# Attention and a feed-forward layer on one core: values of two pairs in one block, three products for the last rows, eight float32 pairs, first loads in another order

## The chip, the core and the metric

The kernel runs on one core of one Trainium2 chip. The metric is the device time of one execution in microseconds (us), before any host work. The engines are named as the profile names them: PE (TensorE, with PEld for its weight loads), DVE (VectorE), ACT (ScalarE), POOL (GpSimd) and SP (SyncE), whose queue issues nearly all transfers.

## The reference

```python
B, H, S, D = 8, 8, 576, 64                       # q, k, v, f
scores = (q @ k^T) / sqrt(D)
cum = cumsum(log(clip(f, 1e-4, 1)))              # per batch and head
scores = where(causal, scores + cum[i] - cum[j], -1e9)
attn = exp(scores - max); attn /= attn.sum() + 1e-9
x = (attn @ v) -> [B*S, H*D] = [4608, 512]
h = x @ w_in                                     # [4608, 2048]
out = (max(h, 0) + alpha * min(h, 0)) @ w_out    # [4608, 512]
```

All is float32. w_in and w_out come as 64-bit numbers, whose conversion on DVE, ACT and POOL is part of the kernel.

## The kernel before

The 64 heads are worked on as 32 pairs, n = 4 b + p: two heads of one batch. A pair's 576 rows are cut into four tiles of 128 rows per head (`tile`, i = 0 to 3, as wide as the causal mask lets them be: 128 (i + 1) columns) and the last 64 rows of each head, which share one set of 128 partitions (`tail`): two groups g of 288 columns.

A score tile goes PE (products into one of 8 PSUM banks) -> DVE (`red`, L628 and L553: adds the mask, scales, takes the row's extreme) -> ACT (exponential with its sum, L518) -> PE (transposes, L531 and L650) -> ACT or DVE (`evac`, L526 and L527: into the tiles eT1, eT2, eT4). `values` (L660 to L680) multiplies them with v: for the rows 0 to 255 (r = 0) and 256 to 575 (r = 1), 64 columns of head 0 into partitions 0 to 63 of a bank and 64 of head 1 into 64 to 127. `quotients` (L587) turns the nine row sums of a pair into reciprocals (L592, L593), transposes them (L596), writes them to DRAM (L602) and reads them back as rows (L604); the fourth pair does this on PE (`quick`). The quotient times the values (L695) is x, which ACT and POOL split into two parts (L697, L699).

Float32 products take several passes of PE. So only the first NN = 6 pairs compute their scores in float32 (`load_0`: tiles q and k of 66 rows, the last two rows of which add the cumulated decay). The later ones use split numbers (`load_n`): KA and QA hold 128 rows, KB and QB 68, so that each product becomes two in a fast format (KA with QA, KB with QB); rounding is done at L424, the remainders on POOL at L474 and L478, and the rows of the decay come from cq in DRAM. Two sets of these four tiles exist (rQ), and one raw q and k (rrq, rrk).

The first feed-forward layer (`ffn1`, b = 0 to 8; b = 8 holds the last 64 rows of all heads) multiplies x of four pairs with w_in in three products each (L726), and ACT and DVE bring the result through four buffers hs to DRAM (L740). w_in is loaded and converted by `load_w_in` and `split64` (L298 to L321). The second layer (`ffn2`, from 741.7 us on) works with seven products in place of eight for blocks of two by two. x tiles are kept in seven buffers (rx).

The order of work is not left to the hardware. Every piece is an `op` with an engine, an expected time, a key and the buffers that it needs. `Plan.run` walks through time and gives each engine the piece that can start first, at equal start the one with the lowest key, and writes out each engine's instructions in this order. Attention has keys of about 10 n, FFN1 1e6: it fills gaps. Each engine, and SP's queue too, works strictly in this order, so a piece that was expected early and comes late holds up what stands behind it. `change_a` frees the memory of the float32 tiles (p0) when their last scores are done and turns it into a second pair of eT1 and eT2 buffers.

Of the kernel before, what the change touches and what calls it, by code (L numbers as in the profile page):

```python
# [18 lines left out]
NP = H // 2  # L19
# [5 lines left out]
NN = 6  # L25
NS = 10
HURRY = 25
CONV0, CONV = 36, 2.2
# [154 lines left out]
def attention_moe(  # L183
# [21 lines left out]
    cq = dram.tile([2, B * H, 2, S], F32, name="cq")  # L205
    c0 = dram.tile([2, 2 * H, S], F32, name="c0")
# [21 lines left out]
    def ring(pool, n, shape, dt, name):  # L228
# [7 lines left out]
    rQ = Ring(Store([(sp.tile([128, QW], F32R, name=f"QA{i}"), sp.tile([68, 1280], F32R, name=f"QB{i}"),  # L236
                      sp.tile([128, 2 * S], F32R, name=f"KA{i}"), sp.tile([68, 2 * S], F32R, name=f"KB{i}"))
                     for i in range(2)]))
# [15 lines left out]
    sel = sp.tile([9, 6, 128], F32, name="sel")  # L254
    mask = sp.tile([128, 928], BF16, name="mask")
    warm = sp.tile([1, 1], F32, name="warm")

# [5 lines left out]
    wbf = p0.tile([128, 512], BF16, name="wbf")  # L263

    def change_a():
        ctx_0.close()
        p1 = ctx_a.enter_context(tc.tile_pool(name="pa", bufs=1, reuse_waits="tile"))
        for r, shape, name in ((rT1, [128, 384], "eT1b"), (rT2, [128, 4, 320], "eT2b")):
            for i in range(2):
                r.store.free.append((plan.t, len(r.store.items)))  # L270
                r.store.items.append(p1.tile(shape, F32, name=f"{name}{i}"))
# [17 lines left out]
    def c_dve(n):  # L289
        return 75 + n / 0.96  # L290
# [114 lines left out]

    o_zero = op("POOL", 400, zeros, -96)
# [23 lines left out]
    def load_0(n, bqk):  # L430
# [3 lines left out]
        ld = [op("SP", 450, lambda: sy.dma_start(bqk.t[0][0:64], qq[b, p, 0:64]), -99 if n < 2 else key, (), [bqk], kb=304),  # L434
              op("SP", 450, lambda: sy.dma_start(bqk.t[1][0:64], kk[b, p, 0:64]), -99 if n < 2 else key, (), [bqk], kb=288)]
# [22 lines left out]
    def load_n(n, bQ):  # L458
# [14 lines left out]
        for i, (a0, a1) in enumerate(pieces(QW, 4)):  # L473
            rdy.append(op("POOL", c_po(a1 - a0), lambda a0=a0, a1=a1: po.tensor_tensor(  # L474
                QA()[64:128, a0:a1], bq.t[64:128, a0:a1], QA()[64:128, a0:a1].bitcast(F32), ALU.subtract),
                kc, [qc[i // 2], qb], [bq, bQ]))
        for i, (a0, a1) in enumerate(pieces(2 * S, 4)):
            rdy.append(op("POOL", c_po(a1 - a0), lambda a0=a0, a1=a1: po.tensor_tensor(  # L478
                KB()[0:64, a0:a1], bk.t[0:64, a0:a1], KA()[0:64, a0:a1].bitcast(F32), ALU.subtract),
                kc, [kc_[i // 2]], [bk, bQ]))  # L480
        q2 = lambda: QB()[66:68].rearrange("p (h s) -> p h s", h=2)[:, :, 0:S].bitcast(F32)
# [5 lines left out]
        return rdy  # L487

    def attention(n):
# [6 lines left out]

        if n >= NN:
            bQ = Buf(rQ)
            rdy, held = [[load_n(n, bQ)] * 2] * 2, [bQ]
# [36 lines left out]
        def tail(st):  # L536
# [3 lines left out]
            for g in range(2):  # L540
# [9 lines left out]
                s = op("PE", 2 * len(qf) * c_s(288), prods, st + 0.6 * g, rdy[0][1] + rdy[1][1], [bS] + held)  # L550

                def red(bS=bS, ks=ks, g=g):
                    ve.tensor_tensor_reduce(out=bt.t[:, ks], in0=bS.t[:, :288], in1=mask[:, 0:288] if g else mask[:, 288:576],  # L553
# [3 lines left out]
                prev = op("DVE", c_dve(288) + 60, red, st + 0.6 * g, [s, o_mask, prev], [bS, bt, bst])  # L557
# [29 lines left out]
        def quotients(key):  # L587
# [3 lines left out]
            def rec():  # L591
                ve.tensor_scalar_add(su(), su(), 1e-9)  # L592
                ve.reciprocal(su(), su())  # L593

            q_ = op("DVE", 160, rec, key, sums, [bst])
# [64 lines left out]
        def values(r, st):  # L660

            bP, w_ = Buf(rP), R[r][1]

            def pv():
                both = []
                for h in range(2):
# [6 lines left out]
                for c, pair in enumerate(zip(*both)):  # L673
                    for h, (j, q0, q1, m) in enumerate(pair):
                        mm(bP.t[64 * h : 64 * h + 64, q0:q1], bv.t[:, j, h], m, c == 0, c == len(both[0]) - 1)

            ns = 3 * c_m4(320) + c_m4(192) + c_m4(64) if r else c_m4(256) + c_m4(128)

            pvo = op("PE", ns + 95, pv, st, e1 + e2[0] + e2[1] + [e4, o_zero, l_v], [bP, bv] + (bT2 + [bT4] if r else bT1))
            xs_ops[r].append(op("ACT", c_act(w_), lambda: ac.activation(bxs[r].t, bP.t[:, :w_], AF.Copy), st, [pvo], [bP, bxs[r]]))  # L680
# [7 lines left out]
        for r in range(2):  # L688
            values(r, k0 + 9.6 - hurry)
        quotients(k0 + 11 - hurry)  # L690
        bx, xo = Buf(rx), []
        for r in range(2):
            t0, w_ = R[r]
            st = k0 + 11.5 - hurry
            mu = op("DVE", c_dve(w_), lambda r=r, t0=t0, w_=w_: ve.tensor_tensor(bxs[r].t, bxs[r].t, bri.t[:, t0 : t0 + w_], ALU.mult),  # L695
                    st, xs_ops[r] + ri_ops, [bxs[r], bri])
            xh = op("ACT", c_acs(256), lambda r=r, t0=t0: ac.activation(  # L697
                bx.t[:, 0, t0 : t0 + 256], bxs[r].t[:, 0:256], AF.Copy), st, [mu], [bxs[r], bx])
            xl = op("POOL", c_po(256), lambda r=r, t0=t0: po.tensor_tensor(  # L699
                bx.t[:, 1, t0 : t0 + 256], bxs[r].t[:, 0:256], bx.t[:, 0, t0 : t0 + 256].bitcast(F32), ALU.subtract), st, [xh], [bxs[r], bx])  # L700
            xo += [xh, xl]
            x_late.extend((mu, xh, xl))
        xt_ops.append(op("SP", 400, lambda: sy.dma_start(xt[p, :, 64 * b : 64 * b + 64], bxs[1].t[:, 256:320]), k0 + 11.6, [mu], [bxs[1]], kb=32))
        x_late.append(xt_ops[-1])
        x_ops[b, p] = [bx] + xo
# [46 lines left out]
    o_one = [op("POOL", 2500, lambda i=i: ones(po, i), 0.5 + i, [s_0[-1]] + x_ops[0, 0][1:]) for i in range(2)]  # L752
# [3 lines left out]
    op("-", 0, change_a, 0, s_0)  # L756
# [292 lines left out]
```

## Time and profile before

| | |
|---|---|
| median of 3 runs | 1105.41 us (1100.49 to 1105.73) |
| profiled execution | 1105.64 us, span 1103.9 us |
| mean granted clock of PE | 0.992 |
| PE busy | 1093.6 us, 99% |
| DVE, ACT, POOL busy | 770.9, 673.0, 267.1 us |
| DMA | 169.54 MB, mean 154 GB/s |

The busy shares say which engine has no room; stretches of 25 us say where this holds, since the attention stage (up to about 600 us) mixes with FFN1 and the last third is the second layer alone. In rows in order of time, two numbers lead: the start and how long the row lasted, and a row joins neighbours of one line and engine under the form of the first. Matrix products overlap at their ends, so the distance between starts is what a product costs, not its own duration.

### The profile page before, as it was taken

The numbers are of one execution on the slowest core, as the hardware profiler recorded it, in microseconds if no ns is written. First come the engines' busy times: TensorE is split into PE (matmuls) and PEld (weight loads), VectorE is DVE, ScalarE is ACT, GpSimd is POOL, SyncE is SP. The second block draws the span as 40 slices with busy tenths as digits, with TensorE's granted clock in tenths as the row PEclk, the third lists the DMA queues.
The fourth block names the chain that finished last, engine by engine and source line by source line (L and its number), as shares of the span: only waits on it lengthen the run. The fifth ranks groups of instructions, "written<-read, shape, count | busy, mean of one in ns | idle before, by whom it ended". The sixth has DMA issues, their size and how long they took to land.

```text
span 1103.9 us, 20650 instructions
## 1 busy us (share of the span) xinstructions
PE 1093.6 (99%) x7281; PEld 953.5 (86%) x7281; DVE 770.9 (70%) x1772; ACT 673.0 (61%) x1580; POOL 267.1 (24%) x340
## 2 busy tenths in 40 slices
PE   8999999999999999999999999999999999999998
PEld 5777878888888888888787888889999999999998
DVE  4887786565555654654532688469989898998994
ACT  4888777677658764774763465555455464646451
POOL 3346574444534533444401000000000000000000
PEclk7999999999999999999999999999999999999999
DMA  4667665646555646565322666454344344443521
GB/s 109 182 183 224 208 194 155 191 139 203 169 168 161 183 150 185 149 185 172 119 71 98 213 210 214 158 183 143 117 152 131 122 130 134 134 134 116 147 65 39
DMA packets 104748, 169.54 MB, mean 154 GB/s; under 512 B 15790, under 2 KB 61637, under 8 KB 104644
## 3 DMA queue, kind: packets, MB, share of 16 engines
q1 hardware_dynamic: 104228, 167.96, 49.5%
q8 instruction: 57, 0.93, 0.4%
q14 instruction: 47, 0.39, 0.1%
q10 hardware_dynamic: 416, 0.27, 0.1%
HBM read 111.04 MB, written 49.04 MB: 145 GB/s over the span
## 4 chain that ended last, share of the span: by engine, by line
PE 97%; DMA 1%; DVE 1%; POOL 0%; issue 0%; SPq 0%; DVEq 0%
PE bank L324 89%; PE bank L531 8%; DMA k<-in_kk_dram 0%; POOL KB L478 0%; DMA rk<-in_kk_dram 0%; PE bank L596 0%; PE bank L650 0%; DMA q<-e 0%; DVE st L592 0%; DVE xs L695 0%; DVE hs L983 0%; DVE es L628 0%; DVE hs L986 0%; DVE hs L985 0%; SPq L337 0%
## 5 line engine op out<-in xcount | busy, mean ns | idle before, releaser
L324 PE MATMUL bank<-xx,wi 128*128 128x512 f32 x1728 | 424.4, 395 | 0.0
L324 PEld LDWEIGHTS bank<-xx,wi 128*128 128x128 f32 x1728 | 318.2, 189 | 61.4
L738 DVE SCALAR_TENSOR_TENSOR hs<-bank,sa,hs 128x512 f32<-128x512 f32 x96 | 71.6, 745 | 82.5 <-ACT hs L736 82.4
L478 POOL TENSOR_TENSOR KB<-rk,KA 64x288 fp32r<-64x288 f32 x104 | 89.1, 878 | 158.9 <-DVE KA L424 102.3
L324 PE MATMUL bank<-wot,xx 128*128 128x256 f32 x1008 | 123.9, 283 | 0.0
L324 PE MATMUL bank<-wi,xx 128*128 128x256 f32 x1008 | 123.9, 283 | 0.0
L324 PEld LDWEIGHTS bank<-wot,xx 128*128 128x128 f32 x1008 | 122.3, 192 | 0.0
L324 PEld LDWEIGHTS bank<-wi,xx 128*128 128x128 f32 x1008 | 122.3, 192 | 0.0
L518 ACT ACTIVATE e<-e,st 128x512 f32<-128x512 f32 (+2 forms) x160 | 109.4, 685 | 14.9 <-DVE st L553 10.0
L736 ACT ACTIVATE hs<-bank,ab 128x512 f32<-128x512 f32 x96 | 65.9, 687 | 71.8 <-PE bank L324 71.0
L628 DVE CUSTOM_DVE_ANT_0 e<-bank,mask 128x512 f32<-128x512 f32 (+1 forms) x128 | 76.7, 620 | 36.5 <-PE bank L324 17.9
L474 POOL TENSOR_TENSOR QA<-rq,QA 64x304 fp32r<-64x304 f32 x104 | 91.4, 910 | 28.6 <-DVE QA L424 27.0
L324 PE MATMUL bank<-KA,QA 128*128 128x288 f32 (+4 forms) x312 | 92.9, 335 | 0.0
L324 PE MATMUL bank<-KB,QB 68*128 68x288 f32 (+4 forms) x312 | 88.1, 316 | 0.0
L628 DVE CUSTOM_DVE_ANT_0 es<-bank,mask 128x256 f32<-128x256 f32 (+1 forms) x128 | 43.6, 353 | 58.7 <-PE bank L324 36.3
L531 PE MATMUL bank<-ident,e 128*128 128x128 f32 x576 | 82.6, 275 | 0.0
L699 POOL TENSOR_TENSOR xx<-xs,xx 128x256 fp32r<-128x256 f32 x64 | 49.1, 786 | 136.9 <-ACT xx L697 133.6
L531 PEld LDWEIGHTS bank<-ident,e 128*128 128x128 f32 x576 | 69.6, 142 | 10.0 <-issue 0.9
L527 ACT ACTIVATE eT<-bank 128x384 f32<-128x384 f32 (+2 forms) x136 | 61.9, 487 | 22.7 <-PE bank L531 20.2
L518 ACT ACTIVATE es<-es,st 128x256 f32<-128x256 f32 (+1 forms) x128 | 57.2, 449 | 26.3 <-DVE st L628 25.4
L942 ACT ACTIVATE xx<-gx 128x1024 fp32r<-128x1024 f32 x48 | 50.8, 1058 | 31.1 <-PE bank L324 15.3
L945 DVE TENSOR_TENSOR xx<-gx,xx 128x1024 fp32r<-128x1024 f32 x48 | 58.6, 1221 | 8.1 <-ACT xx L942 8.1
(136 smaller groups left out, 1740.5 us busy)
## 6 DMA issues: line engine op xcount, KB each, us to landing
hd<-hs SPq DMA_DIRECT2D x144, 256.0 KB
wx<-hd SPq DMA_DIRECT2D x47, 512.0 KB
rq<-in_qq_dram SPq DMA_DIRECT2D x26, 608.0 KB
rk<-in_kk_dram SPq DMA_DIRECT2D x26, 576.0 KB
hr<-hd SPq DMA_DIRECT2D x25, 512.0 KB
vr<-in_vv_dram SPq DMA_DIRECT2D x32, 320.0 KB
wr<-in_w_in_dram SPq DMA_DIRECT2D x16, 512.0 KB
wr<-in_w_out_dram SPq DMA_DIRECT2D x16, 512.0 KB
```

The costliest lines, as they stand in the source:

```text
L324: pe.matmul(o, lhsT, rhs, start=start, stop=stop)
L474: rdy.append(op("POOL", c_po(a1 - a0), lambda a0=a0, a1=a1: po.tensor_tensor(QA()[64:128, a0:a1], bq.t[64:128, a0:a1], QA()[64:128, a0:a1] ...
L478: rdy.append(op("POOL", c_po(a1 - a0), lambda a0=a0, a1=a1: po.tensor_tensor(KB()[0:64, a0:a1], bk.t[0:64, a0:a1], KA()[0:64, a0:a1].bitca ...
L518: ex = op("ACT", c_exp(w), lambda: ac.activation(bt.t[:, :w], bt.t[:, :w], AF.Exp, bias=lo()[:, col : col + 1], scale=-1.0, accum_out=su() ...
L527: return op("ACT", c_act(w), lambda: ac.activation(dst(), src(), AF.Copy), key, deps, [bank] + bufs)
L531: pe.transpose(t[:, c : c + 128], src[:, 128 * j : 128 * j + 128], ident)
L628: ve.tensor_tensor_reduce(out=b1.t[:, :w], in0=bS.t[:, :w], in1=mask[:, 928 - w : 928], scale=-0.125, scalar=3.0e38, op0=ALU.add, op1=ALU. ...
L699: xl = op("POOL", c_po(256), lambda r=r, t0=t0: po.tensor_tensor(bx.t[:, 1, t0 : t0 + 256], bxs[r].t[:, 0:256], bx.t[:, 0, t0 : t0 + 256]. ...
L736: cp = op("ACT", c_act(512), lambda bh=bh, bs=bs, fc=fc: ac.activation(bs.t, bh.t, AF.Relu, scale=ab[:, fc : fc + 1]), -1000, [last, o_sg] ...
L738: cp = op("DVE", c_dve(512), lambda bh=bh, bs=bs, fc=fc: ve.scalar_tensor_tensor(bs.t, bh.t, sa[:, fc : fc + 1], bs.t, ALU.mult, ALU.add), ...
L942: his.append(op("ACT", c_acs(128 * GW * (j1 - j0)), lambda j0=j0, j1=j1, src=src, o_=o_: ac.activation(o_(0, j0, j1), src(), AF.Copy), key ...
L945: rdy.append(op("DVE", c_dve(128 * GW * (j1 - j0)), lambda j0=j0, j1=j1, src=src, o_=o_: ve.tensor_tensor(o_(1, j0, j1), src(), o_(0, j0, ...
```

## The change

- NN goes from 6 to 8: pairs 6 and 7 compute their scores in float32 as well.
- Last rows of a float32 pair: two products of 64 columns, one per head, into partitions 0 to 63 and 64 to 127 of the bank, in place of two products of 128 columns (half of them zeros) that add up.
- Last rows of a split pair: the two KB products of a group become one. X holds the rounded q of the last rows of both heads one below the other, Y the remainders of k of both heads; both are copied within SBUF by SP (four copies). The decay, which was in the rows of KB, is now Z: cumulated decay times 8 of the keys, loaded from c8 with one row for 64 partitions (two loads), turned by ACT into a difference with the queries' (c8q), with the causal mask added by POOL to its last 64 columns. `red` adds Z where it added the mask. There is one set of X, Y, Z, made in `change_a`.
- Values from pair 8 on (NV2): an even pair leaves its values to the next one. Then come three pieces: r = 1 of the first pair, r = 0 of both pairs in one bank, r = 1 of the second. The quotients' loads and x of both follow (`rest`).
- `quotients`: the addition of 1e-9 moves from DVE to ACT, and the plan counts 0.4 us more between the reciprocals and their transpose.
- Loads at the start: q and k of the second pair wait for the scan of f, and their key puts them behind the decay rows of the first; w_in waits for the third pair's first scores (s_0[16]) in place of the second's, and its keys start at 40 in place of 36.
- Memory: one of the two split sets lies where the float32 tiles were, and is there from `change_a` on, with its constant rows written then; eT1 and eT2 have four buffers from the start, e five in place of four, es five in place of three.

```diff
-NN = 6
+NN = 8
+NV2 = 8
...
-CONV0, CONV = 36, 2.2
+CONV0, CONV = 40, 2.2
...
     def change_a():
...
-        for r, shape, name in ((rT1, [128, 384], "eT1b"), (rT2, [128, 4, 320], "eT2b")):
...
+        rQ.store.items.append(split_set(p1, 1))
+        rX.store.free.append((plan.t, 0))
+        rX.store.items.append((p1.tile([128, 128], F32R, name="X"), p1.tile([128, S], F32R, name="Y"), p1.tile([128, S], F32, name="Z")))
...
-        ld = [op("SP", 450, lambda: sy.dma_start(bqk.t[0][0:64], qq[b, p, 0:64]), -99 if n < 2 else key, (), [bqk], kb=304),
+        ld = [op("SP", 450, lambda: sy.dma_start(bqk.t[0][0:64], qq[b, p, 0:64]), -99 if n == 0 else -59 if n == 1 else key, [o_scan] if n else (), [bqk], kb=304),
...
+    def load_x(n, bQ, bX, qc, lo):
+
+        b, p = divmod(n, NP)
+        kc, bh = NS * n - 6, b * H + 2 * p
...
+        for h in range(2):
+            ps = slice(64 * h, 64 * h + 64)
+            rdy.append(op("SP", 400, lambda h=h, ps=ps: sy.dma_start(X()[ps].bitcast(F32), QA()[0:64, 512 + 64 * h : 640 + 64 * h].bitcast(F32)), kc, qc, [bQ, bX], kb=32))
+            rdy.append(op("SP", 400, lambda h=h, ps=ps: sy.dma_start(Y()[ps].bitcast(F32), KB()[0:64, S * h : S * h + S].bitcast(F32)), kc, lo[2 * h : 2 * h + 2], [bQ, bX], kb=147))
+            zz.append(op("SP", 400, lambda h=h, ps=ps: sy.dma_start(Z()[ps], c8[bh + h : bh + h + 1].broadcast_to([64, S])), kc - 4, [o_c8], [bX], kb=147))
+        z1 = op("ACT", c_acs(S), lambda: ac.activation(Z(), Z(), AF.Identity, scale=-1.0, bias=c8q[:, bh : bh + 1]), kc, zz + o_c8q, [bX])
+        rdy.append(op("POOL", 260, lambda: po.tensor_tensor(Z()[:, 512:576], Z()[:, 512:576], mask[:, 224:288], ALU.add), kc, [z1, o_mask], [bX]))
+        return rdy
...
                 def prods(bS=bS, ks=ks, kb=kb):
                     o = bS.t[:, :288]
-                    for i, (q, k) in enumerate(zip(qf, kf)):
-                        mm(o, q()[:, 512:640], k()[:, ks], i == 0, False)
-                        mm(o, q()[:, 576:704], k()[:, kb], False, i == len(qf) - 1)
...
+                    if n < NN:
+                        q, k = qf[0], kf[0]
+                        mm(o[0:64], q()[:, 512:576], k()[:, ks], True, True)
+                        mm(o[64:128], q()[:, 640:704], k()[:, kb], True, True)
+                        return
+
+                    mm(o, qf[0]()[:, 512:640], kf[0]()[:, ks], True, False)
+                    mm(o, qf[0]()[:, 576:704], kf[0]()[:, kb], False, False)
+                    mm(o, bX.t[0], bX.t[1][:, ks], False, True)
...
-            def rec():
-                ve.tensor_scalar_add(su(), su(), 1e-9)
-                ve.reciprocal(su(), su())
-
-            q_ = op("DVE", 160, rec, key, sums, [bst])
+            q_ = op("ACT", 230, lambda: ac.activation(su(), su(), AF.Identity, bias=eps), key, sums + [o_eps], [bst])
+            q_ = op("DVE", 190, lambda: ve.reciprocal(su(), su()), key, [q_], [bst])
+            q_ = op("-", 400, lambda: None, key, [q_])
...
+        if n < NV2:
+            for r in range(2):
+                values(r, k0 + 9.6 - hurry)
+        elif n % 2 == 0:
+            waiting.append((prods_of, copy_v, v_deps, bT1, bT2 + [bT4], bv, rest))
+            return
+        else:
...
+            p1 = op("PE", ns_v[1] + 60, prods1(1, lambda: bP1.t), st, d_, [bP1, bv_] + bT2_)
...
+            copy1(1, bP1, 0, st, p1)
+            p_ = op("PE", 2 * ns_v[0] + 60, first, st, d_ + [p1], [bP, bv, bv_] + bT1 + bT1_)
+            copy1(0, bP, 0, st, p_)
+            copy_v(0, bP, 256, st, p_)
+            p2 = op("PE", ns_v[1] + 60, prods_of(1, lambda: bP2.t), st, d_ + [p_], [bP2, bv] + bT2 + [bT4])
+            copy_v(1, bP2, 0, st, p2)
+            rest1()
+        rest()
...
-        w_ready[fc] = split64(NC4, w_in_v[:, :, fs], lambda: wi[:, fc, 0], lambda: wi[:, fc, 1], CONV0 + CONV * fc, [s_0[8]], [])
+        w_ready[fc] = split64(NC4, w_in_v[:, :, fs], lambda: wi[:, fc, 0], lambda: wi[:, fc, 1], CONV0 + CONV * fc, [s_0[16]], [])
```

More of the change, by code (lines that the diff above doesn't have):

```diff
@@ L267, in change_a @@
         p1 = ctx_a.enter_context(tc.tile_pool(name="pa", bufs=1, reuse_waits="tile"))
[L268 to L271 removed]
+        rQ.store.free.append((plan.t, 1))
+        rQ.store.items.append(split_set(p1, 1))
+        rX.store.free.append((plan.t, 0))
+        rX.store.items.append((p1.tile([128, 128], F32R, name="X"), p1.tile([128, S], F32R, name="Y"), p1.tile([128, S], F32, name="Z")))
     def c_mm(n):
@@ L404, in zeros @@
             po.memset(t[64:128], 0.0)
+    o_eps = op("POOL", 100, lambda: po.memset(eps, 1e-9), -97)
     o_zero = op("POOL", 400, zeros, -96)
@@ L456, in load_0, with load_n @@
         return [(ld + r[0], ld + r[0] + r[1]) for r in rows]
-    def load_n(n, bQ):
+    def load_x(n, bQ, bX, qc, lo):
+        b, p = divmod(n, NP)
+        kc, bh = NS * n - 6, b * H + 2 * p
+        X, Y, Z = ((lambda j=j: bX.t[j]) for j in range(3))
+        QA, KB = (lambda: bQ.t[0]), (lambda: bQ.t[3])
+        rdy, zz = [], []
+        for h in range(2):
[6 more added lines that the diff above has]
+        return rdy
+    def load_n(n, bQ, bX):
         b, p = divmod(n, NP)
@@ L486, in load_n @@
                       kc, oo, [bQ], kb=9))
-        return rdy
+        return rdy, rdy_x
+    waiting = []
     def attention(n):
@@ L658, in tile, with prods_of @@
                             st + 0.31, [t], [bT, bT4])
-        def values(r, st):
-            bP, w_ = Buf(rP), R[r][1]
+        def prods_of(r, out):
             def pv():
                 both = []
+                o = out()
                 for h in range(2):
@@ L687, in attention, with first @@
                     tile(h, i, k0 + 6 * r + 2 * (i - 2 * r) + h)
[L688 to L705, printed above, removed]
+        if n < NV2:
+            for r in range(2):
+                values(r, k0 + 9.6 - hurry)
[3 more added lines that the diff above has]
+        else:
+            prods1, copy1, deps1, bT1_, bT2_, bv_, rest1 = waiting.pop()
+            st = k0 + 9.6 - hurry
+            d_ = deps1() + v_deps()
+            bP1, bP, bP2 = Buf(rP), Buf(rP), Buf(rP)
+            p1 = op("PE", ns_v[1] + 60, prods1(1, lambda: bP1.t), st, d_, [bP1, bv_] + bT2_)
+            def first():
+                prods1(0, lambda: bP.t)()
+                prods_of(0, lambda: bP.t[:, 256:512])()
+            copy1(1, bP1, 0, st, p1)
[6 more added lines that the diff above has]
+        rest()
     w_ready = {}
@@ L751, in attention_moe, with turn_c @@
     o_c2 = op("SP", 400, lambda: sy.dma_start(cq[1, :, :, 0:64], c32()[:, :, S - 64 : S]), 1, [o_cl], [bch], kb=32)
-    o_one = [op("POOL", 2500, lambda i=i: ones(po, i), 0.5 + i, [s_0[-1]] + x_ops[0, 0][1:]) for i in range(2)]
+    o_8c = op("DVE", 500, lambda: ve.tensor_scalar_mul(z(), cu(), 8.0), 0.7, [s_0[7]], [bcu, bz])
+    o_c8 = op("SP", 400, lambda: sy.dma_start(c8, z()), 1, [o_8c], [bz], kb=147)
+    bC = [Buf(rT), Buf(rT)]
+    def turn_c():
+        pe.transpose(bC[0].t[:, 0:64], z()[:, S - 128 : S], ident[0:64, 0:64])
+        pe.transpose(bC[1].t[0:64, 0:64], z()[:, S - 64 : S], ident[0:64, 0:64])
+    o_t = op("PE", 220, turn_c, 0.8, [o_8c, o_id], bC + [bz])
+    o_c8q = [op("ACT", 200, lambda: ac.activation(c8q[64:128, 0:63], bC[0].t[64:128, 1:64], AF.Copy), 0.8, [o_t], [bC[0]]),
+             op("ACT", 200, lambda: ac.activation(c8q[0:64, 0:64], bC[1].t[0:64, 0:64], AF.Copy), 0.8, [o_t], [bC[1]])]
+    o_one = [op("POOL", 2500, lambda: ones(po, 0), 0.5, [s_0[-1]] + x_ops[0, 0][1:])]
     o_sg = op("DVE", 800, signs, 0.6, [o_al, s_0[-1]])
@@ L755, in attention_moe @@
         attention(n)
-    op("-", 0, change_a, 0, s_0)
+    o_one.append(op("POOL", 2500, lambda: ones(po, 1), 0.5, [op("-", 0, change_a, 0, s_0)]))
     for n in range(NN, B * NP):
```

67 lines of the change are left out of this document (50 added, 17 removed).

## The prediction

> **What bounds the kernel now.** I read the page's busy shares, slices and chain first, then stretches by time, and the rows in order of time where a stretch looked odd.
>
> ```profile
> PE 1093.6 (99%) x7281; PEld 953.5 (86%) x7281; DVE 770.9 (70%) x1772; ACT 673.0 (61%) x1580; POOL 267.1 (24%) x340
> PE 97%; DMA 1%; DVE 1%; POOL 0%; issue 0%; SPq 0%; DVEq 0%
> ```
> ```profile
> 0.00:25.00 25.00, 21.26 (x63) 12.50 (x64) 10.10 (x34) 9.30 (x24) 10.58 (x30) 0.74 0.43 101
> 25.00:50.00 25.00, 25.00 (x162) 18.13 (x161) 20.40 (x67) 20.77 (x63) 7.54 (x11) 0.99 0.64 175
> 425.00:450.00 25.00, 25.00 (x143) 19.70 (x144) 10.63 (x27) 13.87 (x36) 13.80 (x18) 1.00 0.54 163
> ```
>
> The first number behind each stretch is its length, the second the busy time of PE, then PEld, DVE, ACT, POOL, the granted clock, the DMA share and GB/s. TensorE is busy in 99% of the span and is 97% of the chain. A busy PE could hide waits, so I look at spacings below: they are those of a full PE. Two places fall short: the first 25 us, and a gap at 162 us that is shown further down.
>
> From about 165 us on there is always FFN1 work to fill with:
>
> ```profile
> 426.92 23.91 PE bank L324 x140
> 500.38 32.03 PE bank L324 x176
> ```
>
> In these pieces of the chain PE runs FFN1 alone for 24 and 32 us in the middle of attention: attention has run as far ahead as its buffers let it. So after 165 us a product less is time less, and latency of attention costs nothing until it eats such a piece. The question is PE work, plus the two places.
>
> **The change part by part.** The sum is made against the profiled execution, 1105.64 us (span 1103.9 and 1.7 around it), 0.2 from the median 1105.41.
>
> *Last rows of split pairs.* One split pair, start us and us of each row:
>
> ```profile
> 200.85 0.33 PE L324 MATMUL bank<-KA,QA 128*128 128x128 f32 x1
> ...
> 201.89 0.43 PE L324 MATMUL bank<-KA,QA 128*128 128x288 f32 x2
> 202.15 0.43 PE L324 MATMUL bank<-KB,QB 68*128 68x288 f32 x2
> 202.42 0.43 PE L324 MATMUL bank<-KA,QA 128*128 128x288 f32 x2
> 202.69 0.42 PE L324 MATMUL bank<-KB,QB 68*128 68x288 f32 x2
> 202.95 0.34 PE L324 MATMUL bank<-KA,QA 128*128 128x384 f32 x1
> ...
> 203.64 1.53 PE L324 MATMUL bank<-xx,wi 128*128 128x512 f32 x6
> ```
>
> Durations overlap, so starts count: eight products take 202.95 - 201.89 = 1.06 us, 0.133 each. The two KB products of a group become one of the same width: 2 x 0.133 less per pair, 24 pairs, **-6.4 us**.
>
> *Pairs 6 and 7 in float32.* The other score products of that split pair are 1.04 us up to 201.89, 0.69 for the four of 384 (202.95 to 203.64) and some 0.92 for the four of 512 by the same slope (0.133 at 288, 0.172 at 384): 2.65. In float32 each product is two instructions:
>
> ```profile
> 38.02 3.19 PE L324 MATMUL bank<-k,q 66*128 66x128 f32 x14
> 41.05 0.38 PE L531 MATMUL bank<-ident,e 128*128 128x128 f32 x2
> ```
> ```profile
> 39.10:41.05 1.95, 1.95 (x10) 1.47 (x9) 1.92 (x11) 1.70 (x8) 1.24 (x2) 1.00 0.68 190
> 41.59:42.24 0.65, 0.65 (x4) 0.34 (x3) 0.65 (x2) 0.27 (x1) 0.00 (x0) 1.00 0.30 104
> 30.77:31.63 0.86, 0.86 (x4) 0.33 (x3) 0.86 (x4) 0.60 (x2) 0.00 (x0) 1.00 0.96 329
> ```
>
> The row of 14 is one product of 128, two of 256 and the last rows, which are the stretch of 1.95. The other stretches are one product of 384 and one of 512. 0.86 for 512 columns is 1.68 ns a column, so the second product of 128, which stands apart, is 0.22. Scores: 0.22 + (3.03 - 1.95) + 2 x 0.65 + 2 x 0.86 = 4.3 us, 1.65 more than split: **+3.3** for two pairs. It also takes 16 POOL pieces (L474, L478) out of the time before pair 8.
>
> *Last rows of float32 pairs.* Two products of 64 columns into the two halves of the partitions replace two of 128. No row of before shows this with q and k; the values have the form:
>
> ```profile
> 43.22:44.17 0.95, 0.95 (x3) 0.19 (x1) 0.95 (x6) 0.95 (x3) 0.95 (x2) 1.00 0.16 35
> 44.17:47.03 2.86, 2.86 (x30) 1.85 (x29) 2.81 (x8) 2.85 (x10) 2.80 (x5) 1.00 0.37 101
> ```
>
> The second stretch is one pair's values, 14 products of 64 columns, 3200 columns in all. At 1.68 ns a column one behind the other would be 5.4 us; it takes 2.86, so the heads run side by side and about 0.15 is lost at the end. The stretch before it holds a product of 512 and takes 0.95 in place of 0.86: 0.09 lost on entering. So the last rows go from 1.95 to 0.98 + 0.24 = 1.22 if both groups stand together as now, 1.46 if apart. Six pairs: -4.4 (or -2.9); pairs 6 and 7 against 1.06: +0.3 (or +0.8). I take **-4.1**. Bounds: -4.4, and +4 if the halves do not overlap (then 2.2 a pair).
>
> The Trainium skill, TensorEngine Tiling (Array Packing), Key Properties, says that a change of tiling mode drains TensorE, which speaks against many short tiled blocks. The 0.09 and 0.15 agree; with a free switch the sum would be 1.9 better for eight pairs.
>
> *Values two by two.* Two pairs already stand together once:
>
> ```profile
> 356.99 0.87 PE L324 MATMUL bank<-eT1b,vr 128*64 128x256 f32 x8
> 357.69 2.11 PE L324 MATMUL bank<-eT2b,vr 128*64 128x320 f32 x16
> 359.63 2.99 PE L324 MATMUL bank<-eT,vr 128*64 128x64 f32 x32
> 362.55 0.55 PE L531 MATMUL bank<-ident,es 128*128 128x128 f32 x3
> ```
>
> 56 instructions in 5.56 us, against 2 x 2.86 and one more entry: 0.25 saved. At most 12 such joints, 3.0; some exist, and the third block needs a bank that ACT must free first (two rP banks at most), so **-2** (0 to -3). Holding pair n's values until n+1 makes attention burstier; the FFN1 pieces of 24 to 32 us above cover it. Two transposes of c cost +0.2.
>
> *First loads.* In the chain and on SP's queue:
>
> ```profile
> 2.02 5.27 DMA k<-in_kk_dram
> 7.36 2.92 DMA q<-e
> ```
> ```profile
> 2.66 0.60 SPq L434 DMA_DIRECT2D q<-in_qq_dram  x1
> 5.41 5.35 SPq L445 DMA_DIRECT2D q<-e  x5
> 10.27 5.19 PE L324 MATMUL bank<-k,q 66*128 66x128 f32 x16 [2.28 <-DMA q<-e]
> ...
> 24.85 0.42 PE L324 MATMUL bank<-k,q 66*128 66x128 f32 x1
> ```
>
> Five small row copies of L445 take 5.35 us of SP, behind the load at 2.66 and its twin for k: 592 KB for pair 1, whose first product starts at 24.85. Moved past the scan and the row copies, the two loads still land some ten us before that. The row copies are then issued one after the other and land by about 8. **-2.3**, the idle time shown; bounds 0 and -2.9 (the chain's DMA piece). At nothing I cost the w_in loads that move back by a pair (s_0[16], 40), the larger rings, c8 and the late memset of the second set: the float32 pairs 4 to 7 keep PE at work over them; without that cover they are rival D.
>
> *The clock at the start and the stall at 162.*
>
> ```profile
> 12.01:25.66 13.65, 13.65 (x37) 9.13 (x36) 6.33 (x24) 5.41 (x17) 0.00 (x0) 0.50 0.36 93
> 165.61:169.02 3.41, 3.41 (x11) 2.78 (x9) 2.44 (x8) 2.43 (x8) 0.00 (x0) 0.50 0.44 151
> 162.44 2.12 DVE L592 TENSOR_SCALAR st<-st 128x9 f32<-128x9 f32 x1
> 163.13 1.40 POOL L699 TENSOR_TENSOR xx<-xs,xx 128x256 fp32r<-128x256 f32 x2
> 164.87 0.28 PE L596 MATMUL bank<-ident,st 128*9 128x128 f32 x1 [2.37 <-DVE st L593]
> ```
>
> After each idle time the granted clock is 0.5 for a while. Without the first gap it may stay up, but pair 0 then waits for its exponentials: -3 to 0, I take **-1.2**. At 162 one DVE addition on 9 columns lasted 2.12 us and ended with POOL's pieces; PE stood 2.37 and then ran 3.41 at half clock: 4.1 in all. The change moves this addition to ACT and lets the order expect 0.4 more. The Trainium skill, SBUF — State Buffer, Who interferes with whom, says that a tensor_scalar can be locked out by GpSimd for a whole instruction; the row agrees, and by that rule ACT is free of it and the whole 4.1 goes, 1.1 more than the sum has.
>
> A new first split pair (8), whose second buffer set and X, Y, Z come only when pair 7's scores are done, stands at the same place. I take **-3** (0 to -4.1).
>
> *What is added.* Per split pair six DMAs on SP, one ACT pass of 128x576 and 64 columns on POOL; for every pair the small ACT pass. ACT and SP have room (13.87 of 25 above; DMA share 0.54). Behind a late Z wait on ACT stand exponentials and the FFN1 copies that free banks; behind X or Y on SP stand FFN1's stores and the quotients' loads; behind the last rows on PE stands everything. No idle PE row after 165 prices this: below 0 (nothing is taken away but DVE's addition), above one more stall like the 4.1. I take **+2**.
>
> Sum: -6.4 + 3.3 - 4.1 - 2 + 0.2 - 2.3 - 1.2 - 3 + 2 = -13.5; 1105.6 - 13.5 = **1092 us**. Its own range, by the bounds of the clock, the stall and the added waits: 1087 to 1098.
>
> **The rivals.** *A: the stall moves.* The work goes, but pair 8's X, Y and Z or pair 7's quotients give PE a gap of the same kind, and the start stays at half clock. For it: at 162 PE stood on a chain through POOL, and POOL still has 8 pieces a pair from there on. Against: POOL no longer has pairs 6 and 7 to split before. Without the -3 and -1.2: 1096; with a second one 1100.
>
> *B: the halves do not overlap* in the float32 last rows, so the change does not do what it says. Against it are the values' 2.86. Eight pairs at 2.2 in place of 1.22: +7.8, 1100.
>
> *C: slower, by the SP queue.* It issues in order. Each split pair adds six copies that wait for DVE, POOL and the one X set, which is free only when the former last rows are reduced. If FFN1's stores stand behind them until all four hs buffers are full, PE stops. A stop of 2.37 us, as at 162, in every third pair is 0.8 a pair, 19 us in all: 1111. It eats the whole gain from 0.56 a pair (13.5 / 24). Against it: SP waits today too, and PE shows none of it:
>
> ```profile
> SPq L740 <- DVE hs L738: 130.7, 62, 5.1
> ```
>
> These are FFN1's stores: 130.7 us in 62 waits, the longest 5.1.
>
> *D: the early stage turns to ACT and DVE.* Between 25 and 50 us they are at 20.77 and 20.40 of 25; with less PE work and later w_in conversions PE might wait. Then five pairs do not save their 0.7 (+3.6), and if the first FFN1 products come half a pair later (a float32 pair is some 12 us by the starts at 24.85 and 38.02), with nothing to fill it, +6: 1102.
>
> **How the numbers follow.** Forecast 0.62, A 0.17, B 0.05, C 0.06, D 0.07, more gain than 1087 0.03. About 0.5% (5.5 us) is what a measurement of this kernel can tell from no change. Faster (under 1100): forecast, the gain beyond, most of A and a third of B: 0.8. Same: the rest of A, B and D: 0.15. Slower: 0.05, most of C. The range, 1087 to 1101, takes in A and B and leaves out C and half of D.
>
> **What would show it.** Right: PE starts near 8 us; the 288-column products per split pair are six; the 66-row ones stand as 66*64 in pairs some ns apart; no half clock near 165; 28-instruction blocks of values become 56 from pair 8 on. Wrong: idle PE with a releaser on X, Y, Z or SP, or PE waiting for ACT's exponentials (L518) before 60 us.

## The result, and the profile after

The changed kernel takes 1085.93 us (median of 4 runs, 1085.57 to 1086.17); the kernel before took 1104.49 (1100.49 to 1105.73) beside it. The ratio is 0.9838, its 95% interval 0.9811 to 0.9864. Predicted were 1092 and a range from 1087 to 1101: the direction was right, and the time lies 1.1 us below the range. The profiled execution took 1085.87 us with a span of 1084.1, against 1105.64 and 1103.9 before.

The page's busy shares and chain of waits, after the change:

```profile
PE 1078.0 (99%) x7235; PEld 933.7 (86%) x7235; DVE 748.3 (69%) x1741; ACT 686.0 (63%) x1630; POOL 255.8 (24%) x349
PE 98%; DMA 1%; SPq 0%; POOL 0%; ACT 0%; DVE 0%; issue 0%; DVEq 0%; POOLq 0%
```

TensorE still bounds the kernel: 15.6 us less busy time, and 98% of the chain in place of 97%. Four stretches, with the columns of the prediction (length, busy time of PE, PEld, DVE, ACT, POOL, clock, DMA share, GB/s):

```profile
0.00:25.00 25.00, 23.18 (x111) 12.56 (x113) 16.37 (x58) 15.51 (x47) 10.63 (x31) 1.00 0.58 144
25.00:50.00 25.00, 25.00 (x182) 17.34 (x179) 18.88 (x62) 22.05 (x69) 6.52 (x9) 1.00 0.63 171
150.00:175.00 25.00, 24.84 (x162) 19.06 (x161) 13.40 (x43) 18.33 (x55) 11.29 (x16) 1.00 0.70 208
425.00:450.00 25.00, 25.00 (x171) 20.02 (x171) 13.20 (x36) 19.03 (x55) 15.66 (x21) 1.00 0.64 195
```

In the first 25 us the clock is 1.00 in place of 0.74, and PE gets through 111 products in place of 63. It stays at 1.00 through 150 to 175 us. (The column counts the time ahead of the clock's first record, here 6.4 us, as full. The warm-up products show what it was there: up to 6.1 us they start 0.43 us apart, behind it 0.22.) SP's queue and PE at the start, in order of time:

```profile
5.41 3.13 SPq L454 DMA_DIRECT2D q<-e  x5
8.58 0.59 SPq L443 DMA_DIRECT2D q<-in_qq_dram  x1
```
```profile
8.42 3.44 PE L332 MATMUL bank<-k,q 66*128 66x128 f32 x18
...
16.44 0.90 PE L332 MATMUL bank<-k,q 66*128 66x128 f32 x5 [0.36 <-DMA q<-c]
```

The five row copies take 3.13 us of the queue in place of 5.35, and the first score products start at 8.42 in place of 10.27, with no idle time of PE ahead of them. Pair 1 then waits 0.36 us for its rows. The waits of PE in the whole execution are these:

```profile
PE bank L395 <- DVE wbf L392: 1.5, 1, 1.5
PE bank L332 <- DMA q<-c: 0.4, 1, 0.4
PE bank L562 <- ACT e L549: 0.2, 1, 0.2
```

The stop of 2.37 us at 162 is gone, and no wait on X, Y or Z has appeared. The stretch there, with the first block of values of two pairs and the last rows of a split pair (the third, pair 10):

```profile
162.85 5.63 PE L332 MATMUL bank<-eT,vr 128*64 128x320 f32 x56
168.42 0.28 PE L632 MATMUL bank<-ident,st 128*9 128x128 f32 x1
...
170.83 0.43 PE L332 MATMUL bank<-KA,QA 128*128 128x288 f32 x2
171.10 0.29 PE L332 MATMUL bank<-Y,X 128*128 128x288 f32 x1
171.23 0.43 PE L332 MATMUL bank<-KA,QA 128*128 128x288 f32 x2
171.49 0.30 PE L332 MATMUL bank<-Y,X 128*128 128x288 f32 x1
171.63 0.34 PE L332 MATMUL bank<-KA,QA 128*128 128x384 f32 x1
```

Six products take 171.63 - 170.83 = 0.80 us where eight took 1.06, as the prediction's 0.133 each has it; 56 instructions of values take 5.57 up to the next start. The last rows of a float32 pair, here pair 1's, are now eight instructions of 64 columns:

```profile
17.92 1.19 PE L332 MATMUL bank<-k,q 66*64 66x288 f32 x8
```

They start two by two, some 0.01 us apart, and the next product starts at 19.04: 1.12 us, where the prediction had 1.22. So the parts are there as predicted. What was not is the size of the gain.

### The profile page after: what moved, and what is told of

Same layout as the page of the kernel before. It is cut to its first block, busy times and chain, and to the rows that moved or that the text cites. A ratio compares the mean times of both kernels' runs of the same rounds, so it can differ in the third digit from the quotient of the medians.

```text
span 1084.1 us, 20791 instructions
## 1 busy us (share of the span) xinstructions
PE 1078.0 (99%) x7235; PEld 933.7 (86%) x7235; DVE 748.3 (69%) x1741; ACT 686.0 (63%) x1630; POOL 255.8 (24%) x349
## 4 chain that ended last, share of the span: by engine, by line
PE 98%; DMA 1%; SPq 0%; POOL 0%; ACT 0%; DVE 0%; issue 0%; DVEq 0%; POOLq 0%
PE bank L332 89%; PE bank L562 8%; DMA c<-e 0%; PE bank L632 0%; PE bank L686 0%; SPq L454 0%; ACT e L549 0%; DMA q<-c 0%; POOL q L373 0%; POOL k L374 0%; POOL mask L382 0%; POOL mask L386 0%; DVE hs L1065 0%; DVE hs L1068 0%; DVE hs L1067 0%
## 5 line engine op out<-in xcount | busy, mean ns | idle before, releaser
L558 ACT ACTIVATE eT<-bank 128x384 f32<-128x384 f32 x240 | 108.1, 486 | 17.1 <-PE bank L562 13.2
L504 POOL TENSOR_TENSOR KB<-rk,KA 64x288 fp32r<-64x288 f32 x96 | 80.1, 853 | 122.8 <-DVE KA L433 52.9
L332 PE MATMUL bank<-eT,vr 128*64 128x320 f32 (+4 forms) x896 | 91.3, 359 | 0.0
L332 PEld LDWEIGHTS bank<-eT,vr 128*64 128x64 f32 x896 | 58.4, 137 | 37.0 <-issue 3.6
L499 POOL TENSOR_TENSOR QA<-rq,QA 64x304 fp32r<-64x304 f32 x96 | 81.9, 884 | 16.3 <-DVE QA L433 14.5
L332 PE MATMUL bank<-KA,QA 128*128 128x288 f32 (+4 forms) x288 | 82.8, 329 | 0.0
```

Of the source, the lines that this page charges most:

```text
L332: pe.matmul(o, lhsT, rhs, start=start, stop=stop)
L558: return op("ACT", c_act(w), lambda: ac.activation(dst(), src(), AF.Copy), key, deps, [bank] + bufs)
```

## The experiments

All changes of a run are told against the changed kernel's 1085.9 (names with a_) or against the runs of the kernel before that were made beside it (names with b_; their median was 1105.57 and 1105.56 beside those here). The kernel before does not always take one time: its runs gather near 1097.4, 1100.4 and 1105.6, and the profiled one belongs to the last group. Each run's mean granted clock goes with its group: 1.000, then 0.996 to 0.998, then 0.992. The time less the share of clock that was lost, time x (1 - clock), is within about 1 us of 1097 in all three, so the clock accounts for the groups.

### What the start is worth: b_warm, b_loads, a_loads, a_cold

b_warm, the kernel before, and a_cold, the changed one, differ only in how long TensorE is kept at work before the first scores (three products to a pass):

```diff
-    for i in range(7):
+    for i in range(10):    # b_warm
...
-    for i in range(7):
+    for i in range(3):     # a_cold
```

b_loads is the kernel before with the two loads of pair 1 held back as in the change; a_loads is the changed kernel with these loads as before (the diff the other way). The line for q is shown, the one for k is alike:

```diff
-        ld = [op("SP", 450, lambda: sy.dma_start(bqk.t[0][0:64], qq[b, p, 0:64]), -99 if n < 2 else key, (), [bqk], kb=304),
+        ld = [op("SP", 450, lambda: sy.dma_start(bqk.t[0][0:64], qq[b, p, 0:64]), -99 if n == 0 else -59 if n == 1 else key, [o_scan] if n else (), [bqk], kb=304),
```

> The kernel before with 30 warm-up products in place of 21, so that PE has work until about 10 us and no idle stretch ahead of its first score products at 10.3; loads unchanged. Theory 1 (the idle stretch drops the granted clock, and half clock from 12 to 25.7 us is what cost most at the start): first products still at 10.3, clock 1.0 from then on, 4 to 5 us faster than before, about 1100.5. Rival (the clock falls because the first pair's products of 66 rows are light work, or pair 0 waits for exponentials anyway): half clock after 12 us again or no gain, 1104 to 1105.

> The kernel before with only the order of the first loads changed. Theory 1: first products near 8.4 us, no half clock at the start, 6.5 to 7 us faster than before, about 1098. Rival (only the wait for the row copies goes, 1.9 us; the half clock stays, or pair 0 waits for exponentials): 1102 to 1103.

> The changed kernel with the first loads in the old order. Theory 1: first products at 10.3 us and half clock behind them, 5 to 7 us slower than the changed kernel, 1091 to 1093. Rival: 2 us slower, 1088, with the clock as in the changed kernel.

> The changed kernel with 9 warm-up products in place of 21: they end near 5.3 us and PE stands idle for 3 us until its first products at 8.4. Theory 1: the clock is at half for some windows of about 3.4 us after 8 us, and the time is 3 to 5 us longer, about 1090. Rival (the idle stretch is not the cause): clock as in the changed kernel from 8 us on, 1086.

Measured: b_warm 1099.12 (12 runs, 1097.3 to 1100.9), 6.4 less than before. b_loads 1096.54 (11 runs, 1096.0 to 1098.1), 9.0 less. a_loads 1101.26, 15.3 more than the changed kernel: eight of its 12 runs lie between 1100.1 and 1102.9, three between 1087.1 and 1089.2, the profiled one at 1097.3. a_cold 1099.26 (nine of 12 runs from 1099.2 to 1100.7, three from 1091.2 to 1095.7), 13.3 more.

The stretches of half clock, first a_loads, then a_cold, then b_warm with its start ahead of them:

```profile
12.35:32.83 20.48, 20.48 (x61) 12.24 (x57) 9.20 (x36) 9.16 (x30) 0.00 (x0) 0.50 0.40 100
```
```profile
9.33:40.05 30.72, 30.72 (x93) 17.09 (x94) 12.82 (x49) 13.52 (x44) 2.33 (x11) 0.50 0.43 109
```
```profile
0.00:25.00 25.00, 23.08 (x102) 14.24 (x103) 14.24 (x51) 13.51 (x39) 10.58 (x30) 1.00 0.61 151
159.19:162.60 3.41, 3.41 (x10) 2.52 (x8) 2.37 (x8) 2.26 (x8) 0.00 (x0) 0.50 0.38 124
```

In a_cold PE shows no idle time within these 30.72 us, yet runs at about half speed. Pair 1's first products and the first row behind the stretch, in a_cold and then in the changed kernel:

```profile
21.66 6.47 PE L332 MATMUL bank<-k,q 66*128 66x128 f32 x18
...
40.37 0.87 PE L562 MATMUL bank<-ident,es 128*128 128x128 f32 x6
```
```profile
16.44 3.51 PE L332 MATMUL bank<-k,q 66*128 66x128 f32 x18 [0.36 <-DMA q<-c]
...
26.35 0.88 PE L562 MATMUL bank<-ident,es 128*128 128x128 f32 x6
```

The same 18 products take 6.47 us in place of 3.51, and the same row comes 14.0 us later at the end of the stretch, which is the whole price of 13.3. A stretch of T us at half clock can cost up to T / 2: 15.4 us here, 10.2 in the profiled run of a_loads, 6.8 for the 13.65 us of the kernel before. b_warm, which takes only this stretch away, gained 6.4. b_loads gained 2.6 more, but not all of it is the idle time: its profiled run has none of the half clock near 160 us that b_warm shows (up to 1.7 us), and its stop for the reciprocals is 1.3 us in place of 2.2:

```profile
0.00:25.00 25.00, 23.54 (x108) 14.64 (x110) 16.44 (x59) 15.30 (x44) 10.58 (x30) 1.00 0.65 169
150.00:175.00 25.00, 25.00 (x161) 20.15 (x161) 12.60 (x34) 16.41 (x45) 14.41 (x18) 1.00 0.61 176
```
```profile
PE bank L596 <- DVE st L593: 1.3, 1, 1.3
```

Among the runs with a clock of 1.000 the idle time is worth about 1 us: b_loads took 1096.5 (median of eight), the kernel before 1097.1 to 1097.8.

Before the first products PE had stood for 2.05 us in a_loads and 2.14 in a_cold:

```profile
10.21 5.07 PE L332 MATMUL bank<-k,q 66*128 66x128 f32 x18 [2.05 <-DMA q<-e]
```
```profile
7.63 5.91 PE L332 MATMUL bank<-k,q 66*128 66x128 f32 x18 [2.14 <-POOL q L373]
```

So it's not a late load that costs 13 to 15 us, but the clock that falls in the idle time. a_cold shows this without any change to the loads: it starts 0.8 us earlier than the changed kernel and is 13.3 us slower. One thing doesn't fit as it stands: four of its 12 runs (1099.2 to 1100.7) are listed with a mean clock of 0.999 or 1.000. A half clock from the start on, which has no record before the first rise and is counted as full, would look like this; these runs were not profiled, so it is not shown.

### The old order of loads without the idle time: a_loadswarm

a_loads with ten passes of three products in place of seven:

```diff
-    for i in range(7):
+    for i in range(10):
```

> The changed kernel with the first loads in the order of before (as a_loads, which took 1101.3) and with ten warm-up passes of three products in place of seven, so that TensorE is at work until the first products can start. Theory 1 (the first loads are worth much because the idle time of some 2 us ahead of the first products makes the clock fall, and a half clock follows): the clock stays at 1.0 and what is left is the later start, +2 to +3 us against the changed kernel, 1088 to 1089. Theory 2 (the old order itself is what costs, by late tiles and waits after the start): still near 1100.

Measured: 1087.52 (5 runs, 1087.0 to 1089.3), 1.6 us more than the changed kernel and 13.7 less than a_loads.

```profile
0.00:25.00 25.00, 23.54 (x104) 12.44 (x104) 14.78 (x54) 13.76 (x41) 10.64 (x31) 1.00 0.59 138
```

The clock is at full from its first record (7.5 us) on, and PE goes from the warm-up into the scores without a wait. Theory 1 holds: of the 15.3 us of the old order, 13.7 are the clock and 1.6 the later start. The three runs of a_loads between 1087.1 and 1089.2 have a_loadswarm's time.

### Does the new form of the float32 last rows keep the clock down: a_wide, a_loadswide

The price of the clock was 6.4 in the kernel before and 13.7 in the changed one. A difference between the two at this place is the last rows in two products of 64 columns. a_wide puts the products of 128 columns back (and the plan's time for them); a_loadswide does so and has the first loads as before too:

```diff
-                        mm(o[0:64], q()[:, 512:576], k()[:, ks], True, True)
-                        mm(o[64:128], q()[:, 640:704], k()[:, kb], True, True)
+                        mm(o, q()[:, 512:640], k()[:, ks], True, False)
+                        mm(o, q()[:, 576:704], k()[:, kb], False, True)
...
```

> The changed kernel with the last rows of the eight float32 pairs as two products of 128 columns that add up, as before the change, in place of two of 64 columns side by side. Theory 1 (the prediction's step: 1.95 us a pair against 1.22): +5.8 us, 1091.8. Theory 2 (the side-by-side form gains less, since a change of tiling drains TensorE around each short block, or its gain lies under waits for ACT and DVE in this stretch): +2 to +3, 1088 to 1089.

> The changed kernel with the first loads in the order of before and with the float32 last rows as two products of 128 columns: both edits undone together. Undone one at a time they cost +15.3 (a_loads) and +5.2 us (a_wide). Theory 1 (the half clock after the idle start lasts long because products of 64 columns side by side do not bring the clock back): the start costs about what it did in the kernel before, 6.4 for the clock and 2 for the idle time, so 1091.1 + 8 = 1099, and the half clock lasts some 14 us as before. Theory 2 (its length has nothing to do with that form): the two add up, 1091.1 + 15 = 1106.

Measured: a_wide 1091.12 (5 runs, 1089.3 to 1093.5), 5.2 more, near the predicted 5.8. Its profiled run (1091.34) has a short stretch of half clock that the changed kernel doesn't have, with no wait of PE ahead of it in the trace:

```profile
65.85:69.27 3.42, 3.42 (x13) 2.29 (x12) 3.25 (x8) 1.80 (x4) 0.00 (x0) 0.50 0.14 27
```

That is up to 1.7 of the 5.2 us, so that the form itself is worth 3.5 or more; the two runs with a clock of 1.000 took 1089.3 and 1089.5, 3.5 more. In the trace the 18 products shown above, from pair 1's first to the next transpose, take 16.48 to 20.46 in a_wide:

```profile
16.48 4.13 PE L332 MATMUL bank<-k,q 66*128 66x128 f32 x18
20.46 0.60 PE L562 MATMUL bank<-ident,e 128*128 128x128 f32 x4
```

That is 3.98 us against 16.44 to 19.79 = 3.35 in the changed kernel: 0.63 a pair, 5.0 for eight. Where the rest goes isn't shown; in the first 25 us PE waits 0.36 us for pair 1's rows when pair 0 is done sooner.

a_loadswide took 1093.2 to 1093.9 in six of 12 runs, 1106.6 to 1108.7 in five, 1098.8 in one; the median of 1096.4 lies between the groups and says little. The profiled run belongs to the second group (1108.5):

```profile
11.07:45.20 34.13, 34.13 (x93) 21.20 (x93) 13.64 (x53) 14.26 (x46) 0.65 (x4) 0.50 0.34 81
```

34.13 us of half clock with the wide form, the longest of all: theory 1, that the new form keeps the clock down, falls. The two groups are some 13.5 us apart, as with a_loads. What sets the length of the half clock stays open, and so does why the price differs between the two kernels.

### The last rows of split pairs: a_dummy, a_tail4

a_dummy multiplies X and Y twice; a_tail4 has four products per group as before, and its pairs load no X, Y, Z. In both the plan counts four products. Of the edits only the products are shown:

```diff
+                    mm(o, bX.t[0], bX.t[1][:, ks], True, True)     # a_dummy
                     mm(o, qf[0]()[:, 512:640], kf[0]()[:, ks], True, False)
```
```diff
-                    mm(o, qf[0]()[:, 512:640], kf[0]()[:, ks], True, False)
-                    mm(o, qf[0]()[:, 576:704], kf[0]()[:, kb], False, False)
-                    mm(o, bX.t[0], bX.t[1][:, ks], False, True)
+                    for i, (q, k) in enumerate(zip(qf, kf)):       # a_tail4
+                        mm(o, q()[:, 512:640], k()[:, ks], i == 0, False)
+                        mm(o, q()[:, 576:704], k()[:, kb], False, i == len(qf) - 1)
```

> The changed kernel with one product more per group of a split pair's last rows: X with Y is multiplied twice into the same bank, the first time to be overwritten, so the output stays as it is. 48 products of 288 columns at the 0.133 us that each took in the trace of before. Theory 1 (TensorE's own work sets the time from 165 us on, and what X, Y and Z bring along in copies and waits lies under it): +6.4 us against the changed kernel, 1092.3. Theory 2 (the time hangs on the copies and waits of X, Y and Z, so that PE has room behind them): +0 to +2, 1086 to 1088.

> The changed kernel with the last rows of split pairs in four products per group as before: no X, Y and Z, none of their six copies, no ACT pass and no POOL piece on Z; all other parts of the change stay. It has the same number of TensorE products as the run with one product more (a_dummy), so the two differ by the price of X, Y and Z alone. The prediction's term for added work and waits was +2 (0 to +4.1). Theory 1 (it is hidden, about 0): 1092.3, the same as a_dummy within 1 us. Theory 2 (it costs what the prediction took, 2): 1090, 2 below a_dummy. Against the changed kernel that is +6.4 or +4.4.

Measured: a_dummy 1093.47 (6 runs, 1092.9 to 1095.9), 7.5 more: theory 1, TensorE has no room. a_tail4 1090.98 (5 runs, 1090.3 to 1091.7), 5.1 more and 2.5 below a_dummy. So X, Y and Z cost 6.4 - 5.1 = 1.3 us by a_tail4 alone, 2.5 by the difference; the second is rather too much, since the profiled run of a_dummy (1095.94) has a stop of its own:

```profile
223.89 1.01 DVE L734 TENSOR_TENSOR xs<-xs,ri 128x256 f32<-128x256 f32 x2 [4.73 <-DMA ri<-rd]
224.82 0.74 DVE L809 SCALAR_TENSOR_TENSOR hs<-bank,sa,hs 128x512 f32<-128x512 f32 x1
...
225.61 0.40 PE L332 MATMUL bank<-Y,X 128*128 128x288 f32 x1 [1.48 <-DVE hs L809]
```

This is rival C's kind of stop, and again not on X, Y or Z: the quotients' rows come late from DRAM, DVE stands 4.73 us before them, FFN1's copy (L809) stands behind that on DVE, and PE waits for the bank that the copy frees. It happened once in this execution.

### Values of two pairs: a_single

```diff
-NV2 = 8
+NV2 = 99
```

> The changed kernel with the values of every pair by themselves (the switch NV2 set past the last pair); all else stays. Theory 1 (the joints save 0.25 us each, 12 of them less those that come about by themselves, as predicted): +2 us (0 to +3), 1088. Theory 2 (values held back let attention come in bursts, which costs what the joints save): 0 or below, 1084 to 1086.

Measured: 1088.13 (5 runs, 1088.0 to 1089.3), 2.2 more. Theory 1; the prediction had 2.

### The addition of 1e-9: b_actadd, a_dveadd

b_actadd is the kernel before with the addition on ACT and the 0.4 us in the plan; a_dveadd the changed kernel with both taken back:

```diff
-            def rec():
-                ve.tensor_scalar_add(su(), su(), 1e-9)
-                ve.reciprocal(su(), su())
-
-            q_ = op("DVE", 160, rec, key, sums, [bst])
+            q_ = op("ACT", 230, lambda: ac.activation(su(), su(), AF.Identity, bias=eps), key, sums + [o_eps], [bst])   # b_actadd; a_dveadd the other way
+            q_ = op("DVE", 190, lambda: ve.reciprocal(su(), su()), key, [q_], [bst])
+            q_ = op("-", 400, lambda: None, key, [q_])
```

> The kernel before with one thing of the change alone: the addition of 1e-9 to the row sums on ACT in place of DVE, and 0.4 us more in the plan between the reciprocals and their transpose. Theory 1 (the stop at 162 us and the half clock after it come from the 2.12 us addition on DVE under POOL's pieces, and both go with it): -3 to -4 us against the kernel before, and no half clock near 165 us. Theory 2 (the stop is due to other things, pair 6's first split tiles or the clock's own doing): 0, and a stretch of half clock near 160 to 170 us remains.

> The changed kernel with the addition of 1e-9 back on DVE and without the 0.4 us that the plan counts between the reciprocals and their transpose. Theory 1 (the addition on DVE is held up by POOL's pieces and stops TensorE when it is late): +1 to +4 us against the changed kernel, 1087 to 1090, with a wait of TensorE for the transpose of the reciprocals in the trace. Theory 2 (with eight float32 pairs POOL is not at work at that place any more, and ACT gets its 32 passes back): 0 to -1, 1085 to 1086.

Measured: b_actadd 1102.55 (11 runs, 1097.4 to 1104.5), 3.0 less by the medians, though the runs gather at 1104.0 to 1104.5 and 1097.4 to 1099.3, five each, so that the ratio of 0.9984 (0.9959 to 1.0009) doesn't tell it from no change. The two traces say more. The stop near 162 is gone and with it its half clock; a stop of 1.6 us stands elsewhere now, at 80 us:

```profile
150.00:175.00 25.00, 25.00 (x168) 21.34 (x166) 15.64 (x50) 21.05 (x65) 14.60 (x19) 1.00 0.61 183
```
```profile
PE bank L325 <- POOL xx L699: 1.6, 1, 1.6
```

The profiled runs differ by 1105.64 - 1104.17 = 1.5 us: theory 1's place is right, and part of its gain may have gone into the new stop. At like clocks the gain is 0 to 1.5: 1097.4 and 1097.7 at 1.000, where the kernel before takes 1097.1 to 1097.8. The addition's place and the plan's 0.4 us were moved together, so which of the two does it isn't shown.

a_dveadd took 1089.3 and 1089.5 in two runs and 1094.2 and 1094.7 in two others, 3.5 and 8.5 more (a fifth of 3800 us is left out). The first two have a clock of 1.000, the others 0.995. The price is theory 1's or more, but not at its place; in the profiled run (1094.2) the longest wait after the start is here:

```profile
41.75 0.65 PE L562 MATMUL bank<-ident,e 128*128 128x128 f32 x4 [0.90 <-ACT e L549]
```
```profile
43.73:53.97 10.24, 10.24 (x35) 5.72 (x36) 5.07 (x17) 6.45 (x21) 0.50 (x1) 0.50 0.28 80
```

PE waits 0.90 us for an exponential, and a half clock of 10.24 us follows, up to 5.1 us, which is what lies between the two groups. PE waits nowhere for the transpose of the reciprocals, so the addition's delay on DVE isn't shown as the cause, and what the 3.5 us consist of stays open.

### Six and seven float32 pairs: a_nn6, a_nn7

```diff
-NN = 8
+NN = 6    # a_nn6; a_nn7 has 7
```

> The changed kernel with six float32 pairs in place of eight (pairs 6 and 7 use split numbers and three products for the last rows; the values are paired from pair 8 on as before this edit). Theory 1 (only TensorE's work counts, the prediction's +1.65 a pair, less the last rows' difference of now 0.8 to 1.2 us): -3 to -4 us against the changed kernel, 1082 to 1083. Theory 2 (the two float32 pairs are the time in which POOL splits the first pairs and the second buffer set comes free; without them TensorE stops near 130 to 170 us as it did at 162 us before): 0 to +6, 1086 to 1092.

> The changed kernel with seven float32 pairs in place of eight. With six it took 1096.5, with TensorE waiting for POOL and ACT's conversions between 125 and 175 us. Theory 1 (what is needed is time for POOL to split the first pairs, which one float32 pair of some 12 us gives in part): 1088 to 1092. Theory 2 (one pair is enough, and TensorE's work is 2 us less): 1084. Theory 3 (the first split pair stands then at an odd place in the pairing of values and of batches): as with six, 1096.

Measured: a_nn6 1096.50 (11 runs, 1094.6 to 1099.6), 10.6 more; a_nn7 1094.16 (10 runs, 1092.8 to 1095.9), 8.2 more. The waits of PE in a_nn6, and then in a_nn7:

```profile
PE bank L332 <- ACT wi L327: 4.1, 3, 2.2
PE bank L562 <- ACT e L549: 2.0, 3, 1.7
...
PE bank L332 <- POOL QA L499: 1.0, 2, 0.5
```
```profile
PE bank L332 <- POOL QA L499: 3.1, 2, 2.0
PE bank L562 <- ACT e L549: 2.3, 3, 1.3
```

With six pairs PE waits for the conversion of w_in and for POOL's pieces of the first split pairs, with seven for the latter, and with both for exponentials; each of the two profiled runs has 6.83 us of half clock between 146 and 164 us. For six, theory 2's cause is in the trace, but the price of 10.6 is above its 6; seven come between theories 1 (at most 1092) and 3 (1096). None of the runs beats the changed kernel.

## Why the prediction was right and where it failed

**What failed: the clock at the start.** The prediction's step was "Without the first gap it may stay up, but pair 0 then waits for its exponentials: -3 to 0, I take -1.2". The clock does stay up, but pair 0 doesn't wait: in the changed kernel PE has 23.18 us of work in the first 25, and its only wait after 8.42 there is 0.36. b_warm measured the term by itself at -6.4. The quoted row would have given it: 13.65 us at half clock are up to 6.8. With -6.4 in place of -1.2, and 1.6 (a_loadswarm) in place of 2.3 for the idle time, the sum is -13.5 - 5.2 + 0.7 = -18.0, 1087.6 us; 1085.9 was measured. The range failed with the same step, since its low end was built on a bound of -3. The runs of the kernel before at a clock of 1.000 say the same: they took 1097.4, 8.2 less than the profiled one with its 13.65 + 3.41 us of half clock, so of the 19.7 us to the changed kernel some 8 are clock.

**The rest of the sum fits in total, not in every term.** b_loads (1096.5) has the first loads and the clock's part, and from there to the changed kernel there are 10.6 us. The prediction's other terms make -13.5 + 2.3 + 1.2 = -10.0. That they come so close is in part luck: 3 of them are for the stall at 162, which in b_loads is a stop of 1.3 us with no half clock, so the other terms gave some 2 us more than was forecast. No run says which; the larger rings and the later w_in loads, which the prediction put at nothing, were not undone apart. One by one:

- *Split last rows*, -6.4, and +2 for added work and waits: 7.5 for as many products put back, 1.3 to 2.5 for X, Y and Z. Both terms held, though no wait of PE in the trace names what the second consists of, and a_dummy's 7.5 is 1.1 above its own products.
- *Float32 last rows*, -4.1 for six pairs and +0.3 for the other two: 3.5 to 5.2 for all eight, against 5.8, so this term was too large. They do run side by side (1.12 us), so rival B is out.
- *Values two by two*, -2: 2.2.
- *Pairs 6 and 7 in float32*, +3.3: as TensorE's work not measured apart. Taken back, they don't give 3.3 but cost 10.6, since the cover is gone that the prediction named. Rival D priced that loss at 3.6 + 6 = 9.6, at the right engines in part, ACT (conversions and exponentials) with POOL in DVE's place, and too early: PE's waits are at 135 to 160 us, not at 25 to 50.
- *The stall at 162*, -3 of 4.1: it is gone from the trace. The addition on DVE with the plan's 0.4 us was its cause (b_actadd, where the stop is gone; b_warm and b_loads keep the addition and still stop for it), but what its removal is worth depends on the next stop: 0 to 1.5 there. Put back, it costs 3.5 or more (a_dveadd), with no wait of PE at its place.

**The rivals.** A did not come: the changed kernel has no stop of its kind and no half clock. C did not come either; a_dummy has shown one stop of its kind, by the quotients' loads. Of "what would show it", all five came: PE at 8.42, six products, products of 64 columns side by side, no half clock near 165, blocks of 56.

## What to carry to other kernels

An idle time of 2 us at the wrong place can cost several times its length in clock: price a stretch of T us at half clock at T / 2 first, and take off only what a row shows to be waiting. Keep TensorE at work up to its first real product; three more warm-up passes alone gave the kernel before 6.4 us. And when an edit adds work on the bounding engine, ask what that work covers before calling it a cost: two pairs at +3.3 us were worth 10.6.

## What the runs showed of the hardware

Every stretch of half clock quoted is a multiple of 3.41 us: 3.41 (b_warm, a_wide), 10.24 = 3 x 3.41, 13.65 = 4 x, 20.48 = 6 x, 30.72 = 9 x and 34.13 = 10 x; and so is the full clock between the two of the kernel before, 165.61 - 25.66 = 41 x 3.41. So the clock is decided in steps of that length. The Trainium skill, TensorE: Matmul & The Clock Gate, Part 1: The HAM clock gate, describes such a window of 3413 ns that runs freely; the traces agree. The first rise of the clock comes at 5.2 us in the trace of the kernel before, at 6.4 in that of the changed one and at 7.5 in a_loadswarm's. So the same idle time can fall into one window in one run and into two in another. That a_loads, a_loadswide and the kernel before take two or three different times goes with each run's clock: the three short runs of a_loads have 0.998 to 1.000, the eight long ones 0.985 to 0.988, and a_loadswide's groups 0.997 to 0.998 and 0.984 to 0.986. That the place of the window is the reason is argued, not shown, since one run of each was profiled.

Unexpected was how long the clock stays down. By the same section the clock falls after a window of idling and one busy window brings it back, and the price of the ramp is below 1% of a typical kernel. Here an idle time of 2.05 to 2.82 us, less than a window, cost 13 to 15 us in the changed kernel, up to 1.4%: PE was busy, as the trace counts it, through six, nine and ten windows at half clock before it rose. Behind the stop at 162 us, with FFN1's products to run, one window was enough. Nor does a stop always lower it: the 1.3 us of b_loads and the 1.6 of b_actadd had no half clock behind them, the 0.90 of a_dveadd had 10.24 us. Which work raises the clock isn't settled; the form of the last rows isn't it.
